# A fused block-causal attention and top-1 mixture of experts: the router's first steps later in the schedule, its squares beside them, one subtraction moved to VectorE

## The chip, the core and the metric

The kernel runs on one core of one Trainium2 chip. The metric is the device time of one launch in microseconds (us), the median over runs. The engines are named as in the profile: PE is TensorE (PEld its weight loads), DVE is VectorE, ACT is ScalarE, POOL is GpSimd, SP is SyncE, which only issues DMAs. PSUM is the memory that PE writes its results to; here it serves as four banks of [128, 2, 512] float32.

## What is computed

Eight batches of 576 tokens, eight heads of 64 go through attention with a block-causal mask; the result, seen as 4608 rows of 512, goes through a router that picks one of eight experts for each row, and through that expert's two matrices.

```python
def _attn_ref(q, k, v):                      # [8, 8, 576, 64] each
    scores = scale * np.matmul(q, k.transpose(0, 1, 3, 2))
    mask = block_i >= block_j                # blocks of 64
    scores = np.where(mask, scores, -1000000000.0)
    scores = scores - np.max(scores, axis=-1, keepdims=True)
    attn = np.exp(scores)
    attn = attn / (np.sum(attn, axis=-1, keepdims=True) + 1e-09)
    return np.matmul(attn, v)
def _moe_ref(x, expert_emb, tau, w1, w2):    # x [4608, 512]
    xn = x / (np.linalg.norm(x, axis=-1, keepdims=True) + 1e-06)
    en = expert_emb / (np.linalg.norm(expert_emb, axis=-1, keepdims=True) + 1e-06)
    logits = xn @ en.T / tau
    expert_idx = np.argmax(logits, axis=1)
    ...
    for e in range(E):
        h = np.maximum(x[mask] @ w1[e], 0.0)
        out[mask] = gate_w[mask, None] * (h @ w2[e])
```

## The kernel before

The launch has two parts. In the first, which lasts to about 365 us, the 64 heads are worked off as 32 pairs (four pairs to a batch) while a router follows batch by batch. In the second the routed rows go through the experts, 128 rows at a time. The change touches the first part alone.

**One pair** is cut into steps by six Python generators. `prep` turns q and k by PE transposes and splits each into a high and a low float32r part (ACT writes `qh` and `kh`, DVE writes `ql` and `kl`). `maxes` multiplies the high parts in four groups; DVE reduces each group to block maxima `nmx` (L367), the last small reduction L374 makes `nmr`, PE turns it and ACT writes `nmT`. `scores` multiplies in five groups and ACT takes the exponential (`pA`, `pT`, L429); POOL adds the probabilities up for the row sums (`pS`, L400 to L403). `values` multiplies with v, and ACT copies the result to `oe` (L463), in two halves. `sums` makes row sums and logits, and ACT copies them to `su` (L502). `finish` turns `su` and `oe` back, and DVE writes the normalised rows `xrow` and the partial logits `lgh`.

**The order** is written out by hand. A string of letters says, for each stretch of the program (one stretch per pair), which generator takes its next step: p, m, s, v, f, l (loads), and r, a step of the router. A steady stretch has 56 letters, 11 of them r. Within an engine the instructions run in the order of these steps. The first stretches, the last five (stretch 27 to 31) and the steady ones have strings of their own.

**The router** of a batch, `route` (L586), starts when `finish` of its fourth pair is done, in stretch 4b+6, and then takes one step at each r. It has 30 steps, so it takes 11 in a first stretch, 11 in a second, 8 in a third; a fourth has none. The document calls these the first, second, third and fourth pair of a route. In the order of its steps: sum of the partial logits `lg` (L594), their maximum `mx` (L596), the subtraction (L598, POOL), the marked candidates `t1` (L601; the profile calls it `t`), their maximum (L603), the one-hot `hot` (L605, with its last rows cleared by L607), then six small matmuls that rank the rows (L616 to L620, called rank here) with the sum `t2` (L725) that reads them, the running count in `hot` (L632); five steps of ACT squares (L582); the square root by POOL (L648); the places in the expert table, and at the end five indirect DMAs that write the table (L672, POOL). Batch 5 (EB) ranks once more for a reserve (`lack`: L625, L627, and the DVE instructions of `reserve`); its route starts in stretch 26, so that its second pair is stretch 27.

**The PSUM banks** go round: `take_bank` pops the first of a list of free banks, `give_bank` appends one. A matmul that takes a bank so waits for the last reader of the bank that was given back longest ago. Which reader that is follows from the order of the steps. In the fourth pair of a route, which holds no router step, the k transposes of `prep` wait for the third reduction of `maxes`, the first group of `scores` for the first reduction, the second group for the copy of the second half of `values`, and the first group of the next `maxes` for `kl`.

Of the kernel before, what the change touches and what calls it, by code (L numbers as in the profile page):

```python
# [8 lines left out]
F32 = mybir.dt.float32  # L9
# [4 lines left out]
ALU = mybir.AluOpType  # L14
# [34 lines left out]
def kernel(  # L49
# [12 lines left out]
    nc = tc.nc  # L62
    B, H, S, D = q.shape
    E, DM, DF = w1.shape
    NT = B * S
    P = 128
    NP = H // 2
    NJ = (S - 64) // P + 1
# [5 lines left out]
    EARLY = 2  # L74
# [36 lines left out]
    def iota(name, shape, pattern, base=0, cm=0, dt=F32):  # L111
        t = const.tile(shape, dt, name=name)
        nc.gpsimd.iota(t, pattern=pattern, base=base, channel_multiplier=cm, allow_small_or_imprecise_dtypes=True)
        return t
# [29 lines left out]
    lim = iota("lim", [P, 1], [[0, 1]], EARLY * P, -EARLY)  # L144
# [37 lines left out]
    def pool(stack, name, bufs, **kw):  # L182
        return stack.enter_context(tc.tile_pool(name=name, bufs=bufs, **kw))
# [3 lines left out]
    sm = pool(right, "sm", 2, side="right")  # L187
# [5 lines left out]
    op = pool(left, "op", 1)  # L193
# [7 lines left out]
    def take_bank():  # L201
        return banks.pop(0) if wide else ps_b.tile([P, 2, 512], F32, name="psb")
# [4 lines left out]
    def give_bank(t):  # L207
        if wide:
            banks.append(t)
# [356 lines left out]
    def store(b, xrow, c0, c1):  # L566
        r0 = b * S + 1
        nc.sync.dma_start(xbuf[r0:r0 + S - 64, c0:c1].rearrange("(j p) w -> p j w", p=P), xrow[:, 0:NJ - 1, c0:c1])
        nc.sync.dma_start(xbuf[r0 + S - 64:r0 + S, c0:c1], xrow[0:64, NJ - 1, c0:c1])
# [10 lines left out]
    def squares(x, o):  # L580
        xs = sm.tile([P, DM], F32, name="xs", bufs=1)
        nc.scalar.activation(xs[:, 0:x.shape[1]], x, AF.Square, accum_out=o)  # L582

    def bc(ap, *shape):
        return ap.to_broadcast(shape)

    def route(b, xrow, lgh, ssp):

        lg = sm.tile([P, NJ, E], F32, name="lg")
        mx = sm.tile([P, NJ], F32, name="mx")  # L590
        t1 = sm.tile([P, NJ, E], F32, name="t1")
        ohb, acc = hot[b % 2][:, 0:NJ, :], hot[b % 2][:, NJ, :]
        eng = nc.gpsimd if b < B - 1 else nc.vector
        nc.vector.tensor_reduce(lg, lgh.rearrange("p j h e -> p j e h"), axis=AX.X, op=ALU.add)  # L594
        yield
        nc.vector.tensor_reduce(mx, lg, axis=AX.X, op=ALU.max)  # L596
        yield
        eng.tensor_tensor(lg, lg, bc(mx.unsqueeze(2), P, NJ, E), op=ALU.subtract)  # L598
        yield

        nc.vector.scalar_tensor_tensor(t1, lg, 0.0, erev, op0=ALU.is_ge, op1=ALU.mult)  # L601
        yield
        nc.vector.tensor_reduce(mx, t1, axis=AX.X, op=ALU.max)  # L603
        yield
        nc.vector.tensor_tensor(ohb, t1, bc(mx.unsqueeze(2), P, NJ, E), op=ALU.is_equal)  # L605
        yield
        nc.vector.memset(ohb[64:P, NJ - 1, :], 0.0)  # L607
        yield

        rb = take_bank() if wide else ps_m.tile([P, 1, 512], F32, name="psm")  # L610
        rk_ps = rb[:, 0]
        rk = rk_ps[:, 0:NJ * E].rearrange("p (j e) -> p j e", e=E)
        if b == B - 1:
            ends.append((rk, ohb))
        yield "pe"
        nc.tensor.matmul(rk, triS, ohb, start=True, stop=False)  # L616
        for j in range(NJ - 1):
            nj = NJ - 1 - j
            nc.tensor.matmul(rk[:, j + 1:NJ, :], onesb, bc(ohb[:, j:j + 1, :], P, nj, E), start=False, stop=False)
        nc.tensor.matmul(rk, onesb, bc(acc.unsqueeze(1), P, NJ, E), start=False, stop=True)  # L620
        if b < B - 1:
            t2 = above(rk, ebase)
            if b == EB:
                c0 = rb[:, 1, 0:NJ + 1]
                nc.tensor.matmul(c0, onesb, hot[b % 2][:, :, 0], start=True, stop=True)  # L625
                lack = sm.tile([P, 1], F32, name="lack")
                nc.vector.tensor_reduce(lack, c0, axis=AX.X, op=ALU.add)  # L627
            give_bank(rb)
        yield
        acc = hot[(b + 1) % 2][:, NJ, :]  # L630
        with nc.allow_low_precision(reason="whole numbers up to 42"):
            nc.vector.tensor_reduce(acc, hot[b % 2].rearrange("p j e -> p e j"), axis=AX.X, op=ALU.add)  # L632
        yield
        if b == B - 1:
            nc.vector.tensor_tensor(accb, acc, early, op=ALU.subtract)
            yield "counted"
        rs = reserve(acc, lack) if b == EB else None

        ss = sm.tile([P, NJ], F32, name="ss")
        gs = sm.tile([P, NJ], F32, name="gs")  # L640
        if b < B - 1:
            for j in range(NJ):
                squares(xrow[:, j, 0:DM], ss[:, j:j + 1])
                rs = drain(rs, 1)
                yield
        else:
            nc.vector.tensor_reduce(ss, ssp, axis=AX.X, op=ALU.add)
        nc.gpsimd.tensor_tensor(ss, ss, half, op=ALU.pow)  # L648
        if b == B - 1:
            yield  # L650
        eng.tensor_scalar(ss, ss, 1.0e-6, None, op0=ALU.add)
        yield
        if b < B - 1:
            rowj = yield from table_rows(t2, ohb)
        nc.vector.reciprocal(ss, ss)
        yield
        eng.tensor_tensor(lg, lg, bc(ss.unsqueeze(2), P, NJ, E), op=ALU.mult)
        yield
        nc.scalar.activation(gx[b % 2][:, :, 0:E], lg, AF.Exp)
        yield  # L660
        nc.vector.tensor_reduce(gs, gx[b % 2], axis=AX.X, op=ALU.add)
        yield
        nc.vector.reciprocal(xrow[:, :, DM:DM + 1], gs.unsqueeze(2))
        yield
        if b < B - 1:
            pieces.extend((b, xrow, j) for j in range(NJ - 1))
        else:
            store(b, xrow, (NP - 1) * P, RW)
        yield
        if b < B - 1:  # L670
            for j in range(NJ):
                w = nc.gpsimd.indirect_dma_start(  # L672
                    out=table, out_offset=bass.IndirectOffsetOnAxis(ap=rowj[:, j:j + 1], axis=0),
                    in_=tokf[:, b, j:j + 1], in_offset=None, bounds_check=E * RE * P - 1, oob_is_err=False)
                for o in writes:
                    tc.declare_no_dep(w.ins, o.ins, reason="each place is written once")
                writes.append(w)
                if (b == B - 2 or j == NJ - 1) and pieces:
                    store_piece()
                yield  # L680
            if b == EB:
                early_g.append(early_rows())

    EB = B - 3
# [5 lines left out]
    def indices(eng, rows, outs, tk, none):  # L690
# [4 lines left out]
        eng.tensor_tensor(none, tk, none, op=ALU.add)  # L695
        eng.tensor_scalar(none, none, -1.0, None, op0=ALU.add)
        eng.tensor_copy(outs, none)

    def reserve(acc, lack):
        yield  # L700
        nc.vector.scalar_tensor_tensor(lack, lack, -1.0, lim, op0=ALU.mult, op1=ALU.add)
        yield
        nc.vector.tensor_scalar(lack, lack, 0.0, float(EARLY), op0=ALU.max, op1=ALU.min)
        yield
        nc.vector.tensor_tensor(acc[:, 0:1], acc[:, 0:1], lack, op=ALU.add)
        yield

    def early_rows():
        et = rt.tile([P, EARLY], F32, name="et")
# [13 lines left out]
    def above(rk, base):  # L723
        t = sm.tile([P, NJ, E], F32, name="t2")
        nc.vector.tensor_tensor(t, rk, base, op=ALU.add)  # L725
        return t
# [13 lines left out]
    def table_rows(t, ohb):  # L740

        row = sm.tile([P, NJ], F32, name="row")
        rowt = sm.tile([P, NJ], I32, name="rowt")
        rowj = sm.tile([P, NJ], I32, name="rowj")
        nc.gpsimd.tensor_tensor(t, t, ohb, op=ALU.mult)
        yield
        nc.vector.tensor_reduce(rowj, t, axis=AX.X, op=ALU.max)
        yield
        nc.vector.tensor_scalar(rowt, rowj, P - 1, None, op0=ALU.bitwise_and)
        nc.vector.scalar_tensor_tensor(row, rowj, 1.0 / P, drop, op0=ALU.mult, op1=ALU.add)  # L750
        yield
        nc.vector.scalar_tensor_tensor(rowj, rowt, float(E * RE) - 1.0 / P, row, op0=ALU.mult, op1=ALU.add)
        yield
        return rowj

    def drain(g, n=None, skip=("pe", "squares", "fine")):
        while g is not None and (n is None or n > 0):
            try:
                while next(g) in skip:
                    pass  # L760
            except StopIteration:
                return None
            n = None if n is None else n - 1
        return g
# [480 lines left out]
    mx = ctx.enter_context(tc.tile_pool(name="mx", bufs=1, reuse_waits="tile"))  # L1245
# [79 lines left out]
    a, b = ea  # L1325
# [201 lines left out]
```

## Time and profile before

| | us |
|---|---|
| three runs | 811.11, 811.66, 809.23 (median 811.11) |
| the profiled execution | 810.42, of it the span of instructions 808.7 |
| busy in the span: PE, DVE, ACT, POOL | 779.2, 604.2, 408.4, 435.7 |
| pairs of batch 1's route, first to fourth | 10.51, 9.62, 11.29, 10.30 |

The profiled execution lies 0.7 us under the median of the runs. A pair is measured from the first matmul of its `values` (L457, `pA`) to that of the next. PE's granted clock is full (1.00) in every stretch looked at. Four pairs, one batch, take some 41.7 us.

### The profile page before, as it was taken

Reading aid. Unit: us, or ns where it says so; the run is one execution under the profiler, and the core shown is the slowest. Engines: PE = TensorE matmul, PEld = TensorE weight load, DVE = VectorE, ACT = ScalarE, POOL = GpSimd, SP = SyncE. Lnnn points to the kernel's source line nnn. Section 1 sums busy time; section 2 is a strip of 40 time slices with the busy share of each in tenths; the row PEclk is TensorE's granted clock in tenths of the full one; section 3 lists DMA queues with packets and bytes.
Section 4 is the critical chain, followed back from the end, with each engine's and each line's share of the span. In section 5 each row is a group of like instructions: output and inputs, shape, how many; then the busy total and the mean of one; then the engine's idle time right before and its main releaser. Section 6 shows DMA issues by size and latency. Waiting matters only on the chain. (4 is left out here: it accounts for less than half of the span.)

```text
span 808.7 us, 23043 instructions
## 1 busy us (share of the span) xinstructions
PE 779.2 (96%) x7160; PEld 627.3 (78%) x7160; DVE 604.2 (75%) x1382; ACT 408.4 (50%) x831; POOL 435.7 (54%) x420
## 2 busy tenths in 40 slices
PE   8999999999999998899999999999999999999997
PEld 3678878787878776668878887788888888888885
DVE  6667878686868776658868777877887778877881
ACT  2566757575757564664744456553533332543222
POOL 7555676767676757772347288784761111661110
PEclk9999999999999999999999999999999999999999
DMA  4745364545454543163845357454441111111111
GB/s 104 169 95 136 84 158 105 147 104 132 101 140 100 141 100 101 29 231 127 297 151 166 100 158 235 152 167 150 148 153 45 55 54 45 38 49 55 54 35 39
DMA packets 141421, 93.95 MB, mean 116 GB/s; under 512 B 118925, under 2 KB 120541, under 8 KB 141260
## 3 DMA queue, kind: packets, MB, share of 16 engines
q1 hardware_dynamic: 133228, 69.74, 31.2%
q0 software_dynamic: 8032, 22.36, 8.7%
q8 instruction: 66, 1.08, 0.6%
q14 instruction: 95, 0.78, 0.3%
HBM read 72.71 MB, written 19.71 MB: 114 GB/s over the span
## 5 line engine op out<-in xcount | busy, mean ns | idle before, releaser
L1175 DVE STREAM_TRANSPOSE pt<-h 32x256 f32<-32x256 f32 x528 | 240.6, 456 | 31.3 <-ACT h L1149 14.1
L367 DVE TENSOR_REDUCE nmx<-psm 128x16 f32<-128x1024 f32 (+2 forms) x128 | 125.6, 986 | 21.4 <-PE psm L361 18.5
L912 POOL TENSOR_TENSOR ring_l<-raw,ring_h 128x1024 f32 (+1 forms) x49 | 116.3, 2406 | 35.7 <-ACT ring_h L907 20.0
L1189 POOL DMA_INDIRECT out_dram<-y,outi x36 | 36.7, 1020 | 176.5 <-ACTq L1061 118.8
L1122 PE MATMUL py<-ring_h,hh 128*128 x272 | 109.3, 402 | 0.7 <-ACT h L1149 0.7
L1122 PE MATMUL py<-ring_l,hh 128*128 x272 | 106.3, 391 | 0.0
L429 ACT ACTIVATE pT<-psm 128x640 f32<-128x640 f32 (+2 forms) x128 | 89.1, 703 | 28.2 <-PE psm L361 16.8
L403 POOL TENSOR_TENSOR pS<-pS,pT 128x640 f32<-128x640 f32 (+2 forms) x93 | 93.5, 1006 | 10.9 <-ACT pT L431 3.2
L1122 PE MATMUL py<-ring_h,hl 128*128 x272 | 88.8, 389 | 0.0
L1122 PE MATMUL ph<-ring_l,xh 128*128 x280 | 86.3, 390 | 0.8 <-POOLq L1073 0.8
L1122 PE MATMUL ph<-ring_h,xh 128*128 x280 | 86.3, 389 | 0.6 <-ACTq L1061 0.6
L457 PE MATMUL psm<-pT,vo 128*64 128x320 f32 (+2 forms) x640 | 76.1, 380 | 1.0 <-issue 1.0
L1188 ACT ACTIVATE y<-py,xg 128x512 f32<-128x512 f32 x34 | 23.4, 689 | 103.5 <-PE py L1122 97.9
L1183 DVE TENSOR_TENSOR hl<-pt,hh 128x512 fp32r<-128x512 f32 x66 | 42.5, 686 | 42.0 <-ACT hh L1181 42.0
L422 PE MATMUL psm<-qh,kh 64*128 64x320 f32 (+4 forms) x384 | 66.5, 341 | 5.9 <-ACT pT L429 3.5
L907 ACT CAST ring_h<-raw 128x1024 f32 (+1 forms) x62 | 61.0, 1050 | 22.1 <-POOLq L1073 11.6
L1181 ACT CAST hh<-pt 128x512 fp32r<-128x512 f32 x66 | 35.5, 590 | 72.1 <-DVE pt L1175 71.7
L1122 PE MATMUL ph<-ring_h,xl 128*128 x280 | 69.2, 389 | 0.0
L457 PEld LDWEIGHTS psm<-pT,vo 128*64 128x64 f32 x640 | 43.2, 137 | 29.3 <-issue 1.9
L1122 PEld LDWEIGHTS ph<-ring_l,xh 128*128 128x128 f32 x280 | 52.5, 188 | 12.1 <-POOLq L1073 1.2
L1122 PEld LDWEIGHTS ph<-ring_h,xh 128*128 128x128 f32 x280 | 52.5, 188 | 11.7 <-ACTq L1061 0.8
L1122 PEld LDWEIGHTS ph<-ring_h,xl 128*128 128x128 f32 x280 | 52.6, 188 | 10.9
(289 smaller groups left out, 1680.7 us busy)
## 6 DMA issues: line engine op xcount, KB each, us to landing
raw<-in_moe_w_dram SPq DMA_DIRECT2D x60, 512.0 KB
qn<-in_q_dram SPq DMA_DIRECT2D x64, 128.0 KB
kn<-in_k_dram SPq DMA_DIRECT2D x64, 128.0 KB
vo<-in_v_dram SPq DMA_DIRECT2D x64, 128.0 KB
xbuf<-xrow SPq DMA_DIRECT2D x28, 260.0 KB
raw<-in_moe_w_dram POOLq DMA_DIRECT2D x4, 512.0 KB
qa<-nmT SPq DMA_DIRECT2D x64, 2.5 KB
xbuf<-xrow SPq DMA_DIRECT2D x7, 130.0 KB
```

Source lines behind the costliest of these rows:

```text
L367: nc.vector.tensor_reduce(m[:, :, f:f + o // w], mt[:, :, 0:o].rearrange("p h (b c) -> p h b c", c=w), axis=AX.X, op=ALU.max, negate=True)
L403: nc.gpsimd.tensor_tensor(o, o, pT[:, :, off[t]:off[t] + w], op=ALU.add)
L422: nc.tensor.matmul(st[0:kw, hh, o:o + c1 - c0], kk[hd[hh], t * P:t * P + kw], qq[hd[hh], 64 + c0:64 + c1], start=(x == 0), stop=(x == len( ...
L429: nc.scalar.activation(pT[:, :, f:f + w] if c0 else pA, st[:, :, 0:w], AF.Exp, scale=scale)
L457: m = nc.tensor.matmul(ob[hh * D:(hh + 1) * D, b0:b0 + q1 - c0], rows(vo, ends_v, n, t)[:, hh, :], pTs[hh][0][:, f0:f0 + q1 - c0] if c0 el ...
L907: return (nc.scalar.copy if eng is nc.scalar else eng.tensor_copy)(piece(ring_h, to, c, half), raw[i][:, c * CW:(c + 1) * CW])
L912: return eng.tensor_tensor(piece(ring_l, to, c, half), raw[i][:, c * CW:(c + 1) * CW], piece(ring_h, to, c, half).bitcast(F32), op=ALU.sub ...
L1122: m = nc.tensor.matmul(out, ac, slots[g]["w", i](r, c * n + off), start=(u == 0 and c == 0), stop=(c == nk - 1 and u == len(turns) - 1))
L1175: nc.vector.transpose(pt[32 * j:32 * j + 32, :, 32 * i:32 * i + 32], h[32 * i:32 * i + 32, :, j, :])
L1181: nc.scalar.copy(sets["hh"][u], pt[:, 4 * u:4 * u + 4])
L1183: nc.vector.tensor_tensor(sets["hl"][u], pt[:, 4 * u:4 * u + 4], sets["hh"][u].bitcast(F32), op=ALU.subtract)
L1189: nc.gpsimd.indirect_dma_start(out=out, out_offset=bass.IndirectOffsetOnAxis(ap=to, axis=0), in_=y, in_offset=None, bounds_check=NT - 1, o ...
```

## The change

For batches 0 to 5 the router begins with six empty steps. Its steps up to the running count stand six r later, and the five squares, which had steps of their own, share the steps from `t1` to rank. Squares, square root and everything behind them keep their place. The subtraction of the maximum runs on DVE for these batches. The reserve of batch 5 is no generator any more; its three DVE instructions stand together behind the running count. Batches 6 and 7 keep their order.

```diff
+        if b <= EB:
+            for _ in range(6):
+                yield
         nc.vector.tensor_reduce(lg, lgh.rearrange("p j h e -> p j e h"), axis=AX.X, op=ALU.add)
         yield
         nc.vector.tensor_reduce(mx, lg, axis=AX.X, op=ALU.max)
         yield
-        eng.tensor_tensor(lg, lg, bc(mx.unsqueeze(2), P, NJ, E), op=ALU.subtract)
+        (nc.vector if b <= EB else eng).tensor_tensor(lg, lg, bc(mx.unsqueeze(2), P, NJ, E), op=ALU.subtract)
         yield
 
         nc.vector.scalar_tensor_tensor(t1, lg, 0.0, erev, op0=ALU.is_ge, op1=ALU.mult)
+        square(0)
         yield
         nc.vector.tensor_reduce(mx, t1, axis=AX.X, op=ALU.max)
+        square(1)
         yield
         nc.vector.tensor_tensor(ohb, t1, bc(mx.unsqueeze(2), P, NJ, E), op=ALU.is_equal)
+        square(2)
         yield
         nc.vector.memset(ohb[64:P, NJ - 1, :], 0.0)
+        square(3)
         yield
...
             give_bank(rb)
+        square(4)
         yield
         acc = hot[(b + 1) % 2][:, NJ, :]
         with nc.allow_low_precision(reason="whole numbers up to 42"):
             nc.vector.tensor_reduce(acc, hot[b % 2].rearrange("p j e -> p e j"), axis=AX.X, op=ALU.add)
-        yield
+        if b > EB:
+            yield
...
-        rs = reserve(acc, lack) if b == EB else None
...
+        if b == EB:
+            nc.vector.scalar_tensor_tensor(lack, lack, -1.0, lim, op0=ALU.mult, op1=ALU.add)
+            nc.vector.tensor_scalar(lack, lack, 0.0, float(EARLY), op0=ALU.max, op1=ALU.min)
+            nc.vector.tensor_tensor(acc[:, 0:1], acc[:, 0:1], lack, op=ALU.add)
+        if EB < b < B - 1:
             for j in range(NJ):
                 squares(xrow[:, j, 0:DM], ss[:, j:j + 1])
-                rs = drain(rs, 1)
                 yield
```

DVE, the first pair of batch 1's route, before, from the first reduction of `maxes` to `kl`:

```order
L367 TENSOR_REDUCE nmx_200<-psm_152 128x2
L594 TENSOR_REDUCE lg<-lgh 128x40
L596 TENSOR_REDUCE mx<-lg 128x5
L345 TENSOR_TENSOR ql_186<-psm_150,qh_183 128x2x5x64
L601 SCALAR_TENSOR_TENSOR t_2116<-lg,erev 128x40
...
L605 TENSOR_TENSOR hot_110<-t_2116,mx 128x40
L367 TENSOR_REDUCE nmx_200<-psm_153 128x2
L607 MEMSET hot_110 64x4
L725 TENSOR_TENSOR t_2209<-psm_153,ebase 128x40
L632 TENSOR_REDUCE hot_109<-hot_110 128x8
L374 TENSOR_REDUCE nmr_202<-nmx_200 128x10
L345 TENSOR_TENSOR kl_192<-psm_150,kh_189 128x2x5x64
```

The same end of the first pair in the changed kernel, and on into the second pair; line numbers of the changed kernel run higher (L604, L606, L608, L611, L614, L617, L620, L731, L647 are `lg`, `mx`, the subtraction, `t1`, its maximum, `hot`, its clearing, `t2` and the running count):

```order
L604 TENSOR_REDUCE lg<-lgh 128x40
L606 TENSOR_REDUCE mx<-lg 128x5
L608 TENSOR_TENSOR lg<-lg,mx 128x40
L611 SCALAR_TENSOR_TENSOR t_2116<-lg,erev 128x40
L374 TENSOR_REDUCE nmr_202<-nmx_200 128x10
L345 TENSOR_TENSOR kl_192<-psm_152,kh_189 128x2x5x64
...
L617 TENSOR_TENSOR hot_110<-t_2116,mx 128x40
L620 MEMSET hot_110 64x4
L345 TENSOR_TENSOR ql_187<-psm_150,qh_184 128x2x5x64
L731 TENSOR_TENSOR t_2327<-psm_152,ebase 128x40
L647 TENSOR_REDUCE hot_109<-hot_110 128x8
L367 TENSOR_REDUCE nmx_199<-psm_151 128x2x8
```

Four router instructions now stand in one piece between the fourth reduction of `maxes` and `nmr`; `hot`, `t2` and the count went to the second pair, ahead of its second reduction. On PE rank stood behind the k transposes of the first pair; in the changed kernel it stands in the second pair between the second group of `maxes` (L361) and the first of `scores` (L422):

```order
L361 MATMUL psm_151<-kh_189,qh_183 128x64 x2
L630 LDWEIGHTS triS
L630 MATMUL psm_152<-hot_110,triS 128x40
...
L634 MATMUL psm_152<-hot_110,onesb 128x40
L422 MATMUL psm_153<-qh_185,kh_191 128x256 x2
```

In stretch 27, which has another string, the second pair of batch 5's route begins with the router step of `hot`. DVE in the changed kernel there, from the last part of `finish` on:

```order
L545 TENSOR_TENSOR lgh<-psm_151,rin 128x16
L617 TENSOR_TENSOR hot_110<-t_5133,mx 128x40
L367 TENSOR_REDUCE nmx_199<-psm_152 128x2
L620 MEMSET hot_110 64x4
L731 TENSOR_TENSOR t_5318<-psm_151,ebase 128x40
L641 TENSOR_REDUCE lack<-psm_151 128x1
L367 TENSOR_REDUCE nmx_199<-psm_150 128x2x8
```

and PE at the same place, from the first two groups of `maxes` on:

```order
L361 MATMUL psm_152<-kh_190,qh_184 128x512 x2
L361 MATMUL psm_150<-kh_190,qh_184 128x448 x2
L361 MATMUL psm_150<-kh_190,qh_184 128x64 x2
L457 MATMUL psm_153<-pA,vo_160 64x256 x2
L630 LDWEIGHTS triS
L630 MATMUL psm_151<-hot_110,triS 128x40
...
L639 MATMUL psm_151<-hot_110,onesb 128x6
L457 MATMUL psm_153<-pT_211,vo_160 64x128 x2
```

Rank, which stood in stretch 26 before, now stands behind the first two matmuls of `values`, and the clearing of `hot` that it reads stands behind a reduction of `maxes` on DVE.

## Rows read from the trace of the kernel before

**Rows 1.** Busy time by stretch: start:end, length, engines busy (instructions), clock, DMA.

```profile
96.72:117.30 20.58, 19.78 (x316) 16.17 (x313) 14.80 (x35) 11.86 (x25) 15.75 (x17) 1.00 0.59 138
107.79:117.30 9.51, 9.51 (x160) 8.04 (x157) 7.19 (x17) 5.93 (x12) 7.48 (x8) 1.00 0.75 155
117.30:127.81 10.51, 10.24 (x166) 8.36 (x162) 8.48 (x25) 6.84 (x15) 6.51 (x7) 1.00 0.58 165
127.81:137.43 9.62, 9.62 (x160) 8.03 (x156) 7.73 (x22) 7.88 (x20) 6.12 (x10) 1.00 0.38 84
137.43:159.02 21.59, 19.89 (x316) 15.96 (x312) 14.73 (x35) 11.85 (x25) 16.18 (x17) 1.00 0.58 141
284.28:294.98 10.70, 10.18 (x161) 8.23 (x157) 8.62 (x26) 6.58 (x15) 6.16 (x8) 1.00 0.44 113
```

**Rows 2.** Timelines of DVE and PE, the pair without router steps: start, duration, instruction.

```profile
114.28 0.23 DVE L374 TENSOR_REDUCE nmr<-nmx 128x10 f32<-128x70 f32 x1
...
116.07 0.27 PE L326 MATMUL psm<-ident,nmr 64*128 64x64 f32 x2
116.18 0.29 PE L326 MATMUL psm<-ident,su 64*128 64x64 f32 x4
...
116.59 0.48 PE L361 MATMUL psm<-kh,qh 64*128 64x512 f32 x2
```

**Rows 3.** Timeline of PE, first pair of batch 1's route; in brackets idle, releaser.

```profile
123.91 0.46 PE L326 MATMUL psm<-ident,kn 64*128 64x64 f32 x8 [0.21 <-DVE nmx L367]
...
124.47 0.18 PE L616 MATMUL psm<-hot,triS 128*128 128x40 bf16 x1
...
124.70 0.30 PE L476 MATMUL psm<-pA,ones 128*32 128x128 f32 x1
```

**Rows 4.** Timeline of DVE, first pair of batch 1's route.

```profile
119.56 0.73 DVE L594 TENSOR_REDUCE lg<-lgh 128x40 f32<-128x320 f32 x1
...
121.17 0.19 DVE L601 SCALAR_TENSOR_TENSOR t<-lg,erev 128x40 f32<-128x40 f32 x1
...
125.20 0.82 DVE L345 TENSOR_TENSOR kl<-psm,kh 128x640 fp32r<-128x640 f32 x1
```

**Rows 5.** Timeline of ACT, the pair without router steps, then the first pair.

```profile
115.73 0.33 ACT L502 COPY su<-psm 128x192 f32<-128x192 f32 x1
...
125.66 0.64 ACT L582 ACTIVATE xs<-xrow 128x512 f32<-128x512 f32 x1
...
126.27 0.32 ACT L502 COPY su<-psm 128x192 f32<-128x192 f32 x1
```

**Rows 6.** Timeline of POOL, the pair without router steps.

```profile
115.30 1.55 POOL L401 TENSOR_TENSOR pS<-pT 128x640 f32<-128x640 f32 x1
```

**Rows 7.** Timelines of DVE, POOL and PEld around batch 6's `t1` and `hot`.

```profile
335.66 0.71 DVE L601 SCALAR_TENSOR_TENSOR t<-lg,erev 128x40 f32<-128x40 f32 x1 [0.37 <-POOL lg L598]
336.64 1.23 DVE L605 TENSOR_TENSOR hot<-t,mx 128x40 bf16<-128x40 f32 x1
...
336.26 1.54 POOL L401 TENSOR_TENSOR pS<-pT 128x640 f32<-128x640 f32 x1
...
338.04 0.10 PEld L616 LDWEIGHTS <-triS 128*128 128x128 bf16 x1 [1.49 <-DVE hot L607]
```

**Rows 8.** Timelines of PE and ACT, second pair of batch 1's route.

```profile
131.00 0.36 PE L422 MATMUL psm<-qh,kh 64*128 64x256 f32 x2
...
130.98 0.41 ACT L463 COPY oe<-psm 128x320 f32<-128x320 f32 x1
```

**Rows 9.** Timelines of PE, DVE and POOL, stretch 27.

```profile
294.98 0.65 PE L457 MATMUL psm<-pA,vo 128*64 128x256 f32 x4
...
308.52 0.55 PE L457 MATMUL psm<-pT,vo 128*64 128x192 f32 x4 [0.96 <-issue]
...
296.21 1.22 DVE L367 TENSOR_REDUCE nmx<-psm 128x2 f32<-128x1024 f32 x1
...
295.06 1.54 POOL L403 TENSOR_TENSOR pS<-pS,pT 128x384 f32<-128x384 f32 x2
```

More of the change, by code (lines that the diff above doesn't have):

```diff
@@ L593, in route, with square @@
         eng = nc.gpsimd if b < B - 1 else nc.vector
+        ss = sm.tile([P, NJ], F32, name="ss")
+        gs = sm.tile([P, NJ], F32, name="gs")
+        def square(j):
+            if b <= EB:
+                squares(xrow[:, j, 0:DM], ss[:, j:j + 1])
+        if b <= EB:
+            for _ in range(6):
+                yield
         nc.vector.tensor_reduce(lg, lgh.rearrange("p j h e -> p j e h"), axis=AX.X, op=ALU.add)
@@ L636, in route @@
             yield "counted"
-        rs = reserve(acc, lack) if b == EB else None
-        ss = sm.tile([P, NJ], F32, name="ss")
-        gs = sm.tile([P, NJ], F32, name="gs")
-        if b < B - 1:
+        if b == EB:
[3 more added lines that the diff above has]
+        if EB < b < B - 1:
             for j in range(NJ):
                 squares(xrow[:, j, 0:DM], ss[:, j:j + 1])
-                rs = drain(rs, 1)
                 yield
-        else:
+        elif b == B - 1:
             nc.vector.tensor_reduce(ss, ssp, axis=AX.X, op=ALU.add)
@@ L697, in indices @@
         eng.tensor_copy(outs, none)
[L699 to L706, printed above, removed]
     def early_rows():
```

## The prediction

> **What bounds the kernel now.** I first read the table of busy time: over the span of 808.7 us PE is busy for 779.2, the next engine, DVE, for 604.2. So time is won or lost where PE stands still or where an instruction is added to it. Then I cut the first part into pairs, from the first `values` matmul of a pair to that of the next, and read busy time by stretch. In the pair without router steps (the fourth of batch 0) PE is busy for all of its 9.51 us; DVE has 7.19, POOL 7.48 [rows 1]. The first pair of batch 1's route takes 10.51, PE idle for 0.27 of it by that view; the second takes 9.62. So a first pair costs 1.00 more than a pair without router steps, a second 0.11 more, and the change moves work from one into the other. The third view is the timeline of PE there. Its idle time stands at one place: the k transposes wait 0.21 for a reduction `nmx` [rows 3], late since `t1` and the other router steps stand among the reductions on DVE. Rank follows; it takes 124.70 − 124.47 = 0.23 [rows 3]. Behind it the copy `su` stands on ACT behind a square, 126.27 − 125.66 = 0.61 later than it could begin [rows 5].
>
> **What the delay takes away.** With rank gone and no router instruction among the reductions, DVE and PE run through most of the first pair as in the pair without router steps. The squares share other steps but keep their places on ACT, so `su` is still 0.61 late. In the pair without router steps the copy starts at 115.73 and lasts 0.33 [rows 5]; 0.61 later it ends at 116.67, and the `su` transposes, which stood at 116.18 [rows 2], come at about 116.71: 0.53 late. Without anything else the first pair would take 9.51 + 0.53 = 10.04, 0.47 less than now.
>
> **What stands there instead.** `lg`, `mx`, the subtraction and `t1` now stand in one piece on DVE between the last reduction and `nmr`. In the pair without router steps `nmr` starts at 114.28 [rows 2], so `lg` starts there. It takes 0.73 [rows 4]; `mx` I estimate at 0.15, a little under the 0.19 of `t1` [rows 4], since neighbours overlap. So the subtraction comes to its turn at about 115.16 and `t1` some 0.1 to 0.2 later. At 115.30 POOL begins the 1.55 us sum L401, right behind L400 [rows 6]; it ends at 116.85.
>
> What such a meeting costs shows in batch 6, at another place. `t1`, which takes 0.19 where POOL is idle [rows 4], took 0.71 from 335.66 and ended at 336.37, 0.11 behind the start of L401, that is, with the end of L400. `hot`, which has both of its inputs from DVE, took 1.23 from 336.64 and ended at 337.87; L401 ended at 336.26 + 1.54 = 337.80. Rank behind it started at 338.04, its weight load idle 1.49 for `hot` [rows 7]. So a small DVE instruction that begins within a POOL sum ends with that sum. I take it that the subtraction ends with L400, at about 115.4, and that `t1` then begins within L401 and ends about 0.07 behind 116.85, at 116.9.
>
> The Trainium skill, page "SBUF — State Buffer", section "Who interferes with whom", says that a DVE instruction with two SBUF inputs contends with a GpSimd instruction that reads SBUF, that whichever issues first keeps the shared ports for the whole instruction, and that a tensor_reduce never contends on trn2. The row of `t1` alone allows another reading, since its releaser was a POOL subtraction that the change takes off POOL: then it would not be held any more, and the sum below would come out at 812.5. By the rule it is held again, and the sum is 816.5; the row of `hot`, which waited for nothing of POOL, agrees with the rule, and I go by it.
>
> What is late next: `nmr` (0.23) stands behind `t1`, then `kl`, 0.82 [rows 4]. `nmr` starts at about 116.85, its first 0.1 overlapping the end of `t1`, and `kl` ends at about 117.8. In the pair without router steps PE turned `nmr` at 116.07 and began the next `maxes` at 116.59 [rows 2]; that matmul takes the bank that `kl` reads. So it starts about 117.8 − 116.6 = 1.2 late. The wait covers the 0.53 of `su`, which is due earlier. First pair: 9.51 + 1.2 = 10.71, 0.20 more than 10.51. Bounds: −0.47 (no hold reaches PE) to +0.35 (`kl` starts 0.15 later). I count it for five batches, 0 to 4. Batch 5's took 10.70 [rows 1], so there it is 0.
>
> **The second pair.** Rank adds 0.23 less what it fills, and it changes the order of the banks: it takes one, so each later matmul of the pair waits for another reader than before. The first group of `scores`, at 131.00 before, now takes the bank that the copy of the second half of `values` gives back; that copy ran from 130.98 to 131.39 [rows 8]. It starts at 131.44 at best, and rank lies in that wait: 0.44 over 131.00. Against the pair without router steps that makes 9.51 + 0.44 = 9.95, against 9.62 of now [rows 1] +0.33. `hot`, its clearing, `t2` and the count add some 0.6 to DVE (three or four of about 0.19 as `t1`), whose 7.73 of 9.62 [rows 1] have room; they are ahead of the reductions that free the k transposes' bank, with about 0.3 to spare there. ACT and POOL get nothing new: POOL loses its subtraction, which nobody waits for then. Bounds: +0.12 (the copy comes earlier and only rank counts, 9.51 + 0.23 = 9.74) to +0.75 (DVE late as well, rival D). No DMA is moved: the table writes keep their steps.
>
> **Batch 5's second pair, stretch 27.** The string differs there. PE's first `values` matmul was at 294.98, and from there to 308.52 PE was never idle [rows 9]. In the changed kernel rank stands behind the first two `values` matmuls, so PE comes to it about 0.24 behind 294.98, at 295.22. It needs the clearing of `hot`, which stands on DVE behind a reduction that ran from 296.21 to 297.43 [rows 9]. `hot` itself stands ahead of that reduction; if it begins within the POOL sums, two of 1.54 together from 295.06 to 296.60 [rows 9], the reduction starts at about 296.65 and ends at 297.9. So rank starts at 297.5 to 297.9, 2.3 to 2.7 late; I take 2.45, between. Rank itself adds 0.23, and the count for the reserve, which waits in the same bank behind `t2`, adds about 0.37, an estimate: `t2` and the start of one more matmul, 0.19 each as the smallest rows here [rows 4]. Together +3.05. Bounds: 0.6 (only rank and the count, if `hot` were early) to 3.4.
>
> **The sum.** 5 × (0.20 + 0.33) = 2.65; batch 5: 0 + 3.05; together +5.7. On the profiled execution's 810.42 that is 816.1. The median of the runs, 811.11, lies 0.7 higher, which gives 816.8; I start from 810.8, between the two, for this and for the rivals: 816.5. The experts' part, bound by PE, starts that much later and keeps its length.
>
> **Rivals.**
> A, the other side: the hold doesn't reach PE. It decides whether `t1` is through before L401 starts at 115.30 [rows 6], or POOL waits for DVE; then `nmr` is there before the `su` transposes at 116.71. For it: `lg` to `t1` would need only about 1.0 from 114.28, so it is a matter of 0.15. Against it: L400 runs right ahead of L401 and holds the subtraction first. First pairs 5 × (−0.47), second pairs 5 × 0.33, batch 5 (10.04 − 10.70) + 3.05: +1.7, 812.5, no change that can be told. The page named above would have POOL wait if DVE issued first.
> B: the pairs shift against the table writes. Batch 0's third and fourth pair took 20.58, batch 1's 21.59 [rows 1], so 1.0 is there to be had per batch if POOL's and PE's order falls as in batch 0. Batches 1 to 4: −4.0 beside the +5.7, 812.5. Against it: nothing in these pairs is changed.
> C: the loss in stretch 27 is given back, since PE has 0.96 of idle at 308.52 [rows 9] and more behind. For it: a wait that ends at a fixed time would absorb the delay. Against it: the work that ends this wait comes after PE's own and moves with it. +5.7 − 3.05: 813.4.
> D: DVE is late in the second pair, and the k transposes wait there as they did in the first, about 0.43 with what the wait draws behind it. 5 × 0.43 = 2.1 more: 818.6. The 0.43 is what is left of the 1.00 of a first pair once rank's 0.23 and some 0.34 of it for `su` are taken off.
> E: A and B together: 808.5, faster.
>
> **How the numbers follow.** A measurement of this kernel tells a difference from 0.3%, 2.4 us; so slower begins at 813.5, faster below 808.7. Chances: forecast 0.55, A 0.12, B 0.11, C 0.07, D 0.10, E 0.05. Slower: forecast and D, and 0.03 of A, B and C, which end within 1 us of the bound: 0.68. Same: the other 0.27 of them. Faster: E, 0.05. The range reaches down to A and B less half a us, 811.8, and up to D plus 1.1 for the upper bounds of the hold and of stretch 27, 819.5; it leaves out E and the outer ends, under 2 in 10. The forecast alone, by the bounds of its terms, is 814.5 to 818.
>
> **What would show it.** Right: in the first pairs of batches 1 to 4 `t1` lasts over 1 us and ends with L401; `nmr` and `kl` follow; the next `maxes` matmul is idle for `kl`; the pairs take about 10.7. In second pairs the first group of `scores` is idle for the copy of `values`, and they take about 9.95. In stretch 27 the weight load of rank is idle for `hot` for 2 us or more, and that pair takes about 3 more. Wrong: `t1` at 0.19 and first pairs near 10.0; second pairs at 9.7, if the copy moves up; or stretch 27 unchanged in length. The forecast falls as a whole if third and fourth pairs, which hold no changed instruction, change their length by more than 0.3 each.

## The result and the profile after

The changed kernel took 819.71 us (median of 6 runs, 817.22 to 821.10), the kernel before 810.22 beside it (6 runs): 1.0112 times as long, 95% interval 1.0091 to 1.0133. It is slower, as forecast; the median lies 0.2 above the upper end of the range, and the loss is 9.5 where the sum gave 5.7. The profiled execution has a span of 818.8 against 808.7, 10.1 more. Cut into the same pairs, that growth is

| part | before | after | growth | forecast |
|---|---|---|---|---|
| first pairs, batches 0 to 4 | 10.51 to 10.52 | 10.77 | +1.28 | +1.0 |
| second pairs, batches 0 to 4 | 9.62 to 9.66 | 9.97 to 10.12 | +2.07 | +1.65 |
| third and fourth pairs, five batches | 106.90 | 107.03 | +0.1 | 0 |
| batch 5, first pair | 10.70 | 10.69 | 0 | 0 |
| batch 5, second pair, and the pair behind it | 24.36 | 30.93 | +6.57 | +3.05 |
| all before, and all behind | | | +0.4 and −0.4 | 0 |

The third and fourth pairs keep their sum, but not their lengths: seven of the ten changed by 0.36 to 0.79, some up, some down.

The view of busy time by stretch, of the changed kernel: the first, the second, and the third and fourth pair of batch 1's route, the two pairs behind batch 5's first, and two pieces of these (columns as in [rows 1]):

```profile
118.67:129.44 10.77, 9.82 (x161) 8.19 (x157) 9.86 (x23) 6.76 (x15) 5.99 (x8) 1.00 0.52 143
129.44:139.41 9.97, 9.94 (x167) 8.24 (x163) 8.04 (x25) 8.18 (x20) 5.87 (x8) 1.00 0.37 83
139.41:159.85 20.44, 19.78 (x315) 16.18 (x313) 14.71 (x34) 11.88 (x25) 15.66 (x17) 1.00 0.56 137
298.83:310.34 11.51, 9.30 (x126) 6.66 (x122) 7.10 (x27) 6.19 (x16) 3.47 (x7) 0.85 0.31 71
310.34:329.76 19.42, 16.77 (x234) 13.15 (x231) 10.32 (x28) 8.97 (x19) 13.37 (x13) 0.82 0.28 70
301.40:305.40 4.00, 3.70 (x23) 2.03 (x24) 2.80 (x13) 0.55 (x3) 1.91 (x4) 0.57 0.44 99
319.50:326.00 6.50, 6.48 (x74) 5.70 (x76) 3.86 (x6) 1.46 (x3) 2.65 (x4) 0.53 0.31 84
```

The reader is to see two things. In the first pair PE's idle time grew from 0.27 [rows 1] to 0.95. And in the last four rows the granted clock is no longer 1.00: from 301.73 to 305.14 and from 318.80 to 325.62 it stood at 0.50, the lower of its two levels, 1.2 GHz.

**The first pair.** The timelines of DVE, POOL and PE, in this order:

```profile
124.94 0.74 DVE L604 TENSOR_REDUCE lg<-lgh 128x40 f32<-128x320 f32 x1
125.72 0.20 DVE L606 TENSOR_REDUCE mx<-lg 128x5 f32<-128x40 f32 x1
125.95 0.32 DVE L608 TENSOR_TENSOR lg<-lg,mx 128x40 f32<-128x40 f32 x1
126.31 1.47 DVE L611 SCALAR_TENSOR_TENSOR t<-lg,erev 128x40 f32<-128x40 f32 x1
127.70 0.21 DVE L374 TENSOR_REDUCE nmr<-nmx 128x10 f32<-128x70 f32 x1
127.84 0.81 DVE L345 TENSOR_TENSOR kl<-psm,kh 128x640 fp32r<-128x640 f32 x1
...
125.48 0.74 POOL L400 TENSOR_TENSOR pS<-pA,pT 128x256 f32<-128x256 f32 x1 [4.54 <-ACT pT L429]
126.18 1.55 POOL L401 TENSOR_TENSOR pS<-pT 128x640 f32<-128x640 f32 x1
...
128.06 0.28 PE L326 MATMUL psm<-ident,nmr 64*128 64x64 f32 x2 [0.95 <-DVE nmr L374]
128.70 0.50 PE L361 MATMUL psm<-kh,qh 64*128 64x512 f32 x2
```

The subtraction begins within L400 and ends, 0.32 later, with it; `t1` begins at 126.31, within L401, and ends at 127.78, 0.05 behind L401's end at 127.73. It does 0.19 of work [rows 4]. The reduction `mx` within L400 took its 0.20, unheld. Behind `t1` stand `nmr`, for which PE waits 0.95, and `kl`, which ends at 128.65; the next `maxes` starts at 128.70, on the bank that `kl` frees.

**The second pair.** The timelines of PE and ACT:

```profile
132.72 0.19 PE L630 MATMUL psm<-hot,triS 128*128 128x40 bf16 x1
...
133.07 0.39 PE L422 MATMUL psm<-qh,kh 64*128 64x256 f32 x2
...
132.61 0.41 ACT L463 COPY oe<-psm 128x320 f32<-128x320 f32 x1
```

The first group of `scores` comes 3.63 behind the pair's start, where before it came 3.19 behind [rows 1, 8]: 0.44, as worked out. It starts 0.05 behind the end of the copy.

**Batch 5's second pair.** The timelines of PE and DVE there, and of PE in the pair behind it:

```profile
301.41 0.18 PE L630 MATMUL psm<-hot,triS 128*128 128x40 bf16 x1 [1.92 <-DVE hot L620]
...
302.00 0.17 PE L639 MATMUL psm<-hot,onesb 128*128 128x6 bf16 x1 [0.29 <-DVE t L731]
302.10 3.86 PE L457 MATMUL psm<-pT,vo 128*64 128x128 f32 x20
...
300.02 1.22 DVE L367 TENSOR_REDUCE nmx<-psm 128x2 f32<-128x1024 f32 x1
301.30 0.06 DVE L620 MEMSET hot<- 64x4 uint32 x1
...
316.26 0.55 PE L457 MATMUL psm<-pT,vo 128*64 128x192 f32 x4 [0.65 <-issue]
...
319.52 0.80 PE L361 MATMUL psm<-kh,qh 64*128 64x448 f32 x4 [1.70 <-DVE ql L345]
```

The same twenty matmuls of `values` in the kernel before:

```profile
295.46 2.33 PE L457 MATMUL psm<-pT,vo 128*64 128x128 f32 x20
```

In the pair behind it PE of the kernel before waits at the two places of 316.26 and 319.52 above. The first wait, 0.96 at 308.52, is in [rows 9]; the second is

```profile
311.12 0.50 PE L361 MATMUL psm<-kh,qh 64*128 64x448 f32 x4 [1.03 <-issue]
```

Rank waits for the clearing of `hot` behind the reduction, as forecast, and the count waits 0.29 more. What was not forecast is the next line: the matmuls behind take 3.86 where they took 2.33, 1.53 more, for most of it at half the clock. A second fall begins at 318.80, within a wait of 1.70 (317.82 to 319.52) in the next pair. PE's busy time there grew from 14.23 to 16.77, while its idle time stayed the same, 2.65 against 2.68: the first of the two waits there fell from 0.96 to 0.65, the second grew from 1.03 to 1.70.

### The profile page after: what moved, and what is told of

It is laid out like the page before. It is cut to its first block, busy times and chain, and to the rows that moved or that the text cites. A ratio compares the mean times of both kernels' runs of the same rounds, so it can differ in the third digit from the quotient of the medians.

```text
span 818.8 us, 23034 instructions
## 1 busy us (share of the span) xinstructions
PE 781.9 (96%) x7160; PEld 630.8 (77%) x7160; DVE 614.8 (75%) x1388; ACT 410.2 (50%) x831; POOL 434.0 (53%) x414
## 5 line engine op out<-in xcount | busy, mean ns | idle before, releaser
L422 PE MATMUL psm<-qh,kh 64*128 64x320 f32 (+4 forms) x384 | 67.3, 344 | 6.3 <-ACT pT L429 2.3
L400 POOL TENSOR_TENSOR pS<-pA,pT 128x256 f32<-128x256 f32 x31 | 22.7, 732 | 80.8 <-ACT pT L429 80.8
```

Source lines behind the costliest of these rows:

```text
L422: nc.tensor.matmul(st[0:kw, hh, o:o + c1 - c0], kk[hd[hh], t * P:t * P + kw], qq[hd[hh], 64 + c0:64 + c1], start=(x == 0), stop=(x == len( ...
```

## The experiments

Times are medians; a ratio is to the kernel before on the same chip, with its 95% interval. The kernels ran on three chips: both of batch 5, halves in the changed kernel and the clearing of `hot` on chip 0; halves in the kernel before, four parts, rank behind the scores and the first combination on chip 10; the subtraction on POOL and the last two combinations on chip 7. A line number of a kernel with more lines runs one or two higher.

**Batch 5 in its old order, and batch 5 alone.**

In the first kernel, with the conditions that answer to it (the old `reserve` is back for batch 5):

```diff
-        if b <= EB:
+        if b < EB:
             for _ in range(6):
                 yield
```

In the second:

```diff
-        if b <= EB:
+        if b == EB:
             for _ in range(6):
                 yield
```

> The change for batches 0 to 4 only; batch 5's router runs in the old order. Theory: of the 10.1 us that the span grew, 6.56 arose in stretches 26 and 27 (24.36 to 30.92), 2.5 of it PE's wait for rank and 4.06 a granted clock of half speed behind that wait. So the time falls by about 6.5 against the changed kernel, to about 813, with a mean clock of 1.000; first pairs stay at 10.77, second pairs at 9.97 to 10.12. Rival: the loss in stretch 27 comes from the earlier batches' shift, or is given back elsewhere; then the time stays above 816 and the clock below 1.

> The change for batch 5 only; batches 0 to 4 in the old order. Theory: pairs of batches 1 to 4 at 10.51 and 9.62 to 9.66 as before; stretches 26 and 27 take about 30.9, with the clock at half speed in two places; about 816.5. Rival: the clock falls only by a chance of the timing in the changed kernel; then only the wait of 2.5 to 3 is paid, about 813, clock 1.000.

Busy time by stretch behind batch 5's first pair (the two pairs that the expectations call stretches 26 and 27), the first kernel:

```profile
298.52:305.96 7.44, 7.44 (x118) 5.69 (x115) 6.04 (x21) 6.30 (x16) 3.47 (x7) 1.00 0.49 110
305.96:322.88 16.92, 14.22 (x234) 10.86 (x231) 10.30 (x28) 8.60 (x19) 13.41 (x13) 1.00 0.32 80
```

and the second:

```profile
294.42:304.44 10.02, 7.80 (x126) 5.95 (x122) 7.11 (x27) 6.16 (x16) 3.46 (x7) 1.00 0.36 81
304.44:323.94 19.50, 16.82 (x233) 13.20 (x231) 10.32 (x28) 8.94 (x19) 13.43 (x13) 0.82 0.27 70
```

With batch 5 in its old order both stretches are as before to 0.01. With batch 5 alone the first is 2.57 longer at full clock: that is the price of rank's place, where 3.05 was forecast. The second is 2.58 longer, by the clock. The pairs of batches 0 to 4 were as expected in both: 10.77 and 9.97 to 10.12 in the first kernel, 10.51 and 9.62 to 9.66 in the second. So the parts are told apart, yet the times were missed: 818.35 (1.0096, 1.0073 to 1.0118) where 813 was expected, and 820.08 (1.0117, 1.0092 to 1.0142) where 816.5 was. The profiled execution of the first, its fastest, has its clock at the lower level for 3.4 us from 358.38, behind a wait of 2.00, and the pair that holds this wait, the last but one, is 1.5 longer. The mean clock over the runs was 0.992 to 0.997 there; in the runs of the kernel before beside it, it was 0.994 to 1.000, 0.997 in the mean. So the profile of the kernel before, at 1.000 from end to end, is not typical of its runs: of 45 on chips 0 and 10, eight had 1.000.

**POOL's sum in two halves, in the changed kernel and in the kernel before.**

```diff
-            nc.gpsimd.tensor_tensor(o[:, :, d:w], pT[:, :, 0:S - QA], pT[:, :, off[1] + d:off[1] + w], op=ALU.add)
+            for c, e in ((d, (d + w) // 2), ((d + w) // 2, w)):
+                nc.gpsimd.tensor_tensor(o[:, :, c:e], pT[:, :, c - d:e - d], pT[:, :, off[1] + c:off[1] + e], op=ALU.add)
```

> The changed kernel, but POOL's longest sum (L401, 1.55 us) is issued as two halves of its columns, in all pairs. Theory: t1 is held only to the end of the POOL instruction that it meets, so it ends about 0.7 earlier, nmr and kl follow, and the first pairs fall from 10.77 to about 10.1 (then bound by the copy su); over six batches about -4, to 815.5. Rival: it is the four DVE instructions themselves, in one piece before nmr, that make the wait; then t1 stays late or the first pairs stay at 10.7 and the time at 819.5.

> The kernel before with POOL's longest sum in two halves, nothing else. It tells how much of the 7 us that the halves gave in the changed kernel is the hold of t1. Theory: in the kernel before no small DVE instruction of batches 1 to 5 meets that sum, so first pairs stay at 10.51 and second pairs at 9.62 to 9.66; only batch 6's one-hot, which was held 1.23 us, gains some 0.7; about 810. Rival: the halves help by themselves, whatever DVE does; then first pairs shorten and the time falls by 4 or more, to 806.

The timelines of DVE, POOL and PE in batch 1's first pair, changed kernel with halves:

```profile
125.01 0.80 DVE L612 SCALAR_TENSOR_TENSOR t<-lg,erev 128x40 f32<-128x40 f32 x1
...
124.87 1.70 POOL L402 TENSOR_TENSOR pS<-pT 128x320 f32<-128x320 f32 x2
...
126.09 0.28 PE L326 MATMUL psm<-ident,nmr 64*128 64x64 f32 x2 [0.28 <-ACT xs L583]
```

`t1` takes 0.80 in place of 1.47, and first pairs fall to 10.10, batch 5's to 10.02: the hold is what lengthened them, not the four instructions as such. PE's idle time falls from 0.95 to 0.28, and that rest the profile puts down to the square on ACT. The time fell to 812.64 (1.0024, 1.0006 to 1.0043), by 7 where 4 was expected; the third and fourth pairs, 103.6 in all in place of 107.0, hold the other 3. In the kernel before, the halves left first and second pairs alone, as expected, but the time fell to 807.91 (0.9974, 0.9960 to 0.9988), since third and fourth pairs took the first of these rows; the second is the pair behind batch 5's second:

```profile
137.13:157.71 20.58, 19.59 (x317) 16.19 (x313) 14.94 (x35) 11.85 (x25) 15.94 (x19) 1.00 0.57 138
297.92:315.99 18.07, 15.45 (x234) 12.35 (x231) 10.30 (x28) 8.69 (x19) 13.57 (x15) 0.91 0.30 75
```

20.58 in place of 21.59 [rows 1]. That is the 1.0 per batch that rival B named, gained by another edit. And the clock fell in the second row, behind a wait of 1.66 for `ql`, in a kernel that holds nothing of the change.

**Four parts, and the first square behind `su`.** The sum is cut into four, and

```diff
         nc.vector.scalar_tensor_tensor(t1, lg, 0.0, erev, op0=ALU.is_ge, op1=ALU.mult)
-        square(0)
         yield
         nc.vector.tensor_reduce(mx, t1, axis=AX.X, op=ALU.max)
+        square(0)
         square(1)
```

> The changed kernel with POOL's longest sum in four parts and the first square moved from t1's step to the next, behind the copy su. Theory: with t1 held 0.4 at most and su not behind a square, the first pairs fall from the 10.10 that the halves gave to about 9.7; against the changed kernel -6 in first pairs alone. Rival: four DVE instructions in one piece ahead of nmr make kl late by themselves (1.3 us from the last reduction to nmr); then the first pairs stay at 10.0 or more.

The timelines of DVE and POOL, and busy time of the first pair:

```profile
124.03 0.45 DVE L613 SCALAR_TENSOR_TENSOR t<-lg,erev 128x40 f32<-128x40 f32 x1
...
123.89 1.98 POOL L403 TENSOR_TENSOR pS<-pT 128x160 f32<-128x160 f32 x4
...
116.40:126.14 9.74, 9.74 (x160) 8.19 (x157) 8.84 (x23) 6.15 (x13) 5.87 (x9) 1.00 0.59 165
```

The hold shrinks with the POOL instruction, 1.47, 0.80, 0.45, and PE has no idle time left. Which of the two edits gave which part of the step from 10.10 to 9.74 wasn't run apart. The second pairs took 0.11 more than in the changed kernel. The time was 808.64 (0.9981, 0.9969 to 0.9993).

**Rank behind the first group of scores.**

```diff
+    if n % 4 == 3:
+        return STEADY[0].replace("rrsssl", "srrssl")
     return STEADY[n % len(STEADY)]
```

> The changed kernel, with rank one place later in the second pairs of batches 0 to 4: behind the first group of scores instead of ahead of it, so that scores takes the bank of the long finished reduction and rank that of the copy. Theory: the second pairs lose only rank's own 0.23 over a pair without router steps: 9.75 in batches 0 and 1 in place of 9.97, 0.2 to 0.3 less in the others; -1.2 in all, not to be told in the time. Rival: DVE, which has hot, t2 and the count ahead of its reductions, makes the second pairs long; then they stay at 9.97 to 10.12.

It took 823.14 (1.0156, 1.0136 to 1.0176); the second pairs rose to 11.05, above both expectations; of the two it is the rival's reason, a late DVE, that shows. The timelines of PE and DVE there:

```profile
136.00 0.46 PE L328 MATMUL psm<-ident,kn 64*128 64x64 f32 x8 [0.30 <-DVE nmx L369]
...
138.60 0.28 PE L328 MATMUL psm<-ident,nmr 64*128 64x64 f32 x2 [0.36 <-DVE nmr L376]
...
136.84 1.42 DVE L760 SCALAR_TENSOR_TENSOR rowj<-rowt,row 128x5 int32<-128x5 int32 x1
```

The first group of `scores` did come at its old place, 3.19 behind the pair's start. But `t2`, and with it the reductions behind it on DVE, came later; the k transposes waited 0.30 for one (the wait of the prediction's rival D), and the router's small DVE instructions behind it fell into the next POOL sum: one that works on 128x5 numbers took 1.42, and `nmr` stood behind it.

**The clearing of `hot` ahead of the reduction in stretch 27.**

```diff
-    "rmmvrrvmvvvvrvvspvsrmpsrrrsrvfmvsvrrmrmfflsprrrfvvvrvmmrsfsffrrpvppsspvvppvmvssrrmrmvrvvmmrsmrsrmmsfrfsffssfprrrsmlvfprm",
+    "rrmmvrvmvvvvrvvspvsrmpsrrrsrvfmvsvrrmrmfflsprrrfvvvrvmmrsfsffrrpvppsspvvppvmvssrrmrmvrvvmmrsmrsrmmsfrfsffssfprrrsmlvfprm",
```

> The changed kernel, but in stretch 27 the router's second step comes two places earlier in the string, so that the clearing of hot stands ahead of the 1.22 us reduction on DVE. Theory: rank waits about 0.8 in place of 1.92, the clock stays at full speed as it did behind waits of 0.9 to 1.0 elsewhere; -1.2 for the wait and -4 for the clock, about 814.3. Rival: the clock falls there whatever the length of the wait; then only -1.2, about 818.3, with a mean clock of 0.993 as now.

PE there:

```profile
300.15 0.18 PE L630 MATMUL psm<-hot,triS 128*128 128x40 bf16 x1 [0.79 <-DVE hot L620]
...
301.51 0.17 PE L639 MATMUL psm<-hot,onesb 128*128 128x6 bf16 x1 [1.06 <-DVE t L731]
```

Rank waits 0.79 in place of 1.92, but now `t2` stands behind the same reduction, and the count waits 1.06 for it: the wait was cut in two and only 0.36 was gained. The clock did not fall behind these two waits; it did in the next pair (0.82). The time was 819.16 (1.0117, 1.0089 to 1.0145). That is far from the 814.3 of the theory and near the 818.3 of the rival; but the rival's reason, a clock that falls at this place whatever the length of the wait, isn't what the profile shows.

**The subtraction back on POOL.**

```diff
-        (nc.vector if b <= EB else eng).tensor_tensor(lg, lg, bc(mx.unsqueeze(2), P, NJ, E), op=ALU.subtract)
+        eng.tensor_tensor(lg, lg, bc(mx.unsqueeze(2), P, NJ, E), op=ALU.subtract)
```

> The changed kernel with the subtraction of the maximum back on POOL for all batches. In POOL's order it then stands behind three sums of the same pair (L400, L401 and the first L403). Theory: it starts when the first L403 ends, at 129.35 in the pair where t1 now ends at 127.8; t1, nmr and kl follow it, so each first pair is about 2 longer than 10.77 and the time about 12 longer, 831. Rival: POOL takes it up while those sums wait for the exponential, or the hold alone counts and t1, now 0.2 long behind the sums, makes up for it; then first pairs stay within 0.5 of 10.77.

The timelines of DVE, POOL and PE in batch 1's first pair, and busy time of the first and second pair:

```profile
130.96 0.20 DVE L611 SCALAR_TENSOR_TENSOR t<-lg,erev 128x40 f32<-128x40 f32 x1 [3.65 <-POOL lg L608]
...
130.67 0.25 POOL L608 TENSOR_TENSOR lg<-lg,mx 128x40 f32<-128x40 f32 x1
...
131.44 0.37 PE L326 MATMUL psm<-ident,nmr 64*128 64x64 f32 x2 [2.94 <-DVE nmr L374]
...
120.05:133.55 13.50, 10.56 (x160) 8.85 (x156) 8.60 (x22) 7.14 (x16) 7.54 (x9) 0.89 0.45 130
133.55:145.33 11.78, 11.78 (x164) 9.09 (x162) 7.66 (x25) 7.88 (x18) 4.96 (x8) 0.83 0.31 70
```

`t1` is unheld, 0.20, since POOL is through; but the subtraction waited for three sums, and PE waits 2.94. Within each of the six such waits the clock falls, for 6.8 us or more, and the second pairs, which hold no other change, take 11.8. It took 826.93, with the kernel before at 793.96 beside it (1.0392, 1.0359 to 1.0424). The expectation was 2 for each first pair, where it is 2.7, and 12 in all; the clock was not in it. The changed kernel wasn't run on this chip, but its ratio on its own was 1.0112: so with the delay, VectorE is the better place for the subtraction, and the hold of `t1` costs less than POOL's queue.

**Combinations.** Batches 0 to 4 as changed with the sum in four parts, the first square later and rank behind the first group of scores, batch 5 in its old order:

> Batches 0 to 4 as in the changed kernel with all three mends (the sum in four parts, the first square later, rank behind the first group of scores), batch 5 in its old order. Theory: first pairs at 9.7, second pairs at 9.8, against 10.51 and 9.65 before: 0.65 less per batch, five batches, -3.2, and 0.7 from batch 6's one-hot: about 807, clock 1.000. Rival: what is won in these pairs comes back in the third and fourth, where the table writes fall; then 810 or more.

It took 810.99 (1.0016, 0.9996 to 1.0037) where 807 was expected: first pairs 9.75, but second pairs 10.4 to 10.66, by the move of rank. Its clock fell in the pair behind batch 5's second (0.82), with batch 5 in its old order. Without the move of rank, and the kernel before with the sum in four parts:

> Batches 0 to 4 as changed, with the sum in four parts and the first square later, batch 5 in its old order; rank stays ahead of scores. From the pairs measured so far: first 9.75, second 10.08 to 10.23, stretches 26 and 27 at 24.4 in place of 27.7; against the changed kernel with quarters and later squares -2.3 and no fall of the clock in stretch 27: about 806. Rival: the third and fourth pairs, or the clock in the last stretches, take it back; 808.5 or more.

> The kernel before with POOL's longest sum in four parts. The kernel before with halves took 0.26% less than the kernel before, of it 0.5 in batch 6's one-hot and 4 in third and fourth pairs (20.5 in place of 21.6). If those came from shorter holds, quarters give as much or a little more, about 807.5, third and fourth pairs at 20.5. If they came from the place at which the table writes fall, they may be gone: 810.

They took 793.29 (0.9983, 0.9967 to 0.9999) and 793.59 (0.9991, 0.9975 to 1.0006), with the kernel before at 793.96. By ratio that is nearer to the rival of the first (808.5 or more in place of 806) and to the second reading of the other (810 in place of 807.5). These runs were made on chip 7, and there the kernel before was some 16 faster than on the other chips; whether it is the chip or the time of the run wasn't tried. Batch 1's first, second, and third and fourth pairs of the kernel without the move of rank:

```profile
114.65:124.41 9.76, 9.76 (x161) 8.19 (x157) 8.87 (x23) 6.15 (x13) 5.88 (x9) 1.00 0.74 198
124.41:134.49 10.08, 9.96 (x166) 8.25 (x163) 8.26 (x25) 8.77 (x22) 7.30 (x13) 1.00 0.36 81
134.49:153.53 19.04, 19.04 (x317) 16.11 (x313) 14.60 (x34) 11.93 (x25) 16.54 (x22) 1.00 0.62 148
```

First and second pairs are as in the other runs; the third and fourth took 19.02 to 19.06 in all three kernels of this chip, here without any idle time. So the 1.70 for which PE stands idle in 21.59 of the kernel before [rows 1] was there on the other chips and not on this one, and four parts in the kernel before gave nothing here. Whether it comes from the table writes, which POOL issues in these pairs, stays open; their own durations are the same on chip 7 and in the profile of the kernel before, 0.97 to 1.16.

Three kernels lie 0.2 to 0.3% below the kernel before: this one (0.9983), the changed kernel with four parts and the later square (0.9981), and the kernel before with halves (0.9974). Compared like with like, the delay itself gains nothing that can be told: 793.29 with it and 793.59 without it, both with the sum in four parts on one chip.

## Why the prediction was right, and where it was too small

**First pairs, right.** The forecast had `t1` end with L401, then `nmr`, `kl` and the next `maxes`, 10.71; it was 10.77, with each step in its place; in all six first pairs `t1` took 1.47 and ended 0.05 to 0.06 behind L401. The Trainium skill, page "SBUF — State Buffer", section "Who interferes with whom", has a VectorE instruction with two SBUF inputs contend with a GpSimd instruction that reads SBUF, and a reduction never; the rows agree, 1.47 and 0.20 within sums of the same pair. The other reading of the row of `t1` in batch 6, that it had waited for POOL's subtraction, fell: here nothing of POOL's is its input. Rival A's 10.04 needed `t1` through in time; halves gave 10.10 and quarters with the square moved 9.74. That the square costs was right as well: behind the hold it didn't show, and with halves PE waits 0.28 for it.

**Second pairs, right in place, low in size.** The bank did pass to the copy, +0.44 at the first group of `scores`, and batches 0 and 1 took 9.97 (forecast 9.95). In batches 2 to 4 it was 10.12; the term was +0.33 for each and measured +0.35 to +0.46. That the other bank would give back 0.2, as I took it when I moved rank behind the scores, was not borne out: the pairs lost 0.9 to 1.1 by it, and the k transposes waited for DVE, which the prediction had given 0.3 to spare.

**Batch 5, right in its wait, and the step that failed.** The term of +3.05 measured 2.57 (batch 5 alone). PE came to rank 0.66 behind the pair's start, where 0.24 was taken, so that the wait was 1.92 in place of 2.45. The step that failed is that this term priced a wait by its length alone and left the clock at nothing: the sum has "batch 5: 0 + 3.05" and no more. In the changed kernel's profile the clock went to its lower level twice, 1.53 and 2.54, together 4.07 of the 10.1. (The experts' part did keep its length, as the prediction said: from the end of the pair behind batch 5's second to the end of the launch it is 489.0, and 489.4 before.) The first fall followed the wait for `hot` directly. The second began within a wait of 1.70 for `ql`, which was 1.03 before. It was not there in the first experiment, but was in a combination with batch 5 in its old order (0.82) and in the kernel before with halves (0.91). So batch 5's rank is not needed for it, and that the change caused it is not shown; what lengthens that wait is open.

In the runs the clock's share is smaller than in this pair of profiles. The mean clock was 0.994 in the runs of the changed kernel and 0.997 in those of the kernel before on chips 0 and 10, half the distance of the two profiles, 0.993 and 1.000. By these numbers I estimate the clock at some 2 of the 9.5.

**Rivals.** B happened in part, and the other way as well: third and fourth pairs together went between 20.4 and 22.4 in the changed kernel. The prediction had named as its last sign that it falls as a whole if these pairs change by more than 0.3 each, and seven of ten did. Their sum came out level, 107.03 against 106.90. That is luck: the single lengths moved though nothing in these pairs was changed, and with halves their sum fell by 3.5. C did not: nothing in the stretch absorbed the wait. D was not seen in the changed kernel, and was in the one with rank later. The ends of the range don't follow from the words beside them: 818.6 and 1.1 make 819.7, not 819.5, and half a us below 812.5 is 812.0, not 811.8.

**What stays open.** The two halves of the change, measured apart, cost 7.2 and 9.0, together 9.5. Their profiles show 3.4 in the pairs of the one, and 2.6 of wait and 2.6 of clock in the other; the rest lies in the clock's falls and in the last stretches before the experts, which differ from run to run, and wasn't settled.

## What to carry to other kernels

Before a small VectorE instruction with two inputs in SBUF is moved, look at what GpSimd runs at its new place: it may last as long as the GpSimd instruction that it meets, and so does everything queued behind it. A shorter GpSimd instruction shortens that hold; 1.55 us cut into four took it from 1.47 to 0.45. And a wait of TensorE is priced by its length and by what the clock does behind it.

## What was not expected of the hardware

The granted clock fell to its lower level around waits of PE of 1.65 to 2.94 us, from inside the wait to 1.6 us behind its end: 1.70 and 1.92 in the changed kernel, 2.00, 2.46 and 2.60 in three others, 2.94 six times over with the subtraction on POOL, the rest between 1.65 and 1.93. It stayed there for 3.4 us or more, 6.8 in several, 10.2 in one. It did not fall at each: waits of 1.64, 1.69, 1.92, 2.15 and 2.56 in other profiles passed without, and the same wait for `hot`, 1.92, did both. Between the pairs it never fell at a shorter one, of which the profiles hold many, 0.8 to 1.6. In one profile it fell at 21 us too, where no wait since the first matmul had been over 0.68. The two falls of the changed kernel cost 1.53 and 2.54, about as much as the waits beside them. The mean granted clock of one and the same kernel, the one before, went from 0.993 to 1.000 from run to run on chips 0 and 10, its times from 806.7 to 816.5; on chip 7 it took 792.1 to 797.8 at 0.994 to 1.000.
